# One pool of eight PSUM banks in a fused attention and feed-forward kernel, with the scores in two visits per half batch

## The chip, the cores and the metric

The kernel runs on one core of a Trainium2 chip. The metric is the device time of one launch in microseconds, as the median of several runs. A profile shows one execution; its span runs from the first to the last instruction, some 1.8 us less than the device time.

## The reference, cut to what matters

Attention with a few global and 96 local positions and a linear distance bias, then a feed-forward layer with a squared ReLU:

```python
scores = (q @ k.T) / sqrt(D) + bias          # B, H, S, D = 4, 8, 768, 64
scores = where(is_global | is_local, scores, -1e9)
a = softmax(scores)                          # n_global = 8, n_local = 96
x = (a @ v).transpose(0, 2, 1, 3).reshape(B * S, H * D)      # 3072 x 512
out = square(maximum(x @ w_in, 0)) @ w_out   # 512 -> 2048 -> 512
```

## The kernel before

The kernel works in eight half batches of 384 rows. While TensorE (PE in the profile) does the two feed-forward layers of one half batch, it does the attention of the next between them. Its results go to the banks of PSUM, eight in all in this program: `sp` are scores, `av` is attention times v, `hps` and `yps` are the sums of layer 1 and layer 2, `trp` and `trx` are transposes. ACT takes the exp of scores (`ex`), DVE multiplies by a mask (`phat`), both empty the layers' sums. An attend job is the attention times v of one pair of heads, a load is a DMA transfer into the core, and a filler is a matmul on zeros that the planner puts into gaps of the opening. The first 45 us, until the first layer-2 matmul, are called the opening here: loads arrive, and the first batch is done tile by tile.

The program's order is made ahead of time by a small planner. It is given each job with a cost and what it needs, and emits instructions in the order in which they could start. PSUM stood in two pools, which the planner took each in rotation:

```python
ps_big = ctx.enter_context(tc.tile_pool(name="ps_big", bufs=6, space=bass.MemoryType.PSUM))
ps_att = ctx.enter_context(tc.tile_pool(name="ps_att", bufs=2, space=bass.MemoryType.PSUM))
plan = Plan(1.0, 24.0)
big, att = Ring(6), Ring(2)      # av, trp, trx take att; scores and both layers take big
```

A unit of scores is 8 matmuls of 64 rows into two banks, one for each head of a pair. A half batch has 5 or 6 units. A job of two units took four banks of the ring of six:

```python
TOGETHER = [[[0, NPAIR], [1, 2], [3]], [[0, 1], [2, 3], [4, 5]]]

def score(x, k):
    ...
    units = [UNITS[x.half][u] for u in TOGETHER[x.half][k]]
    ...
    job = plan.pe(0.182 + 0.062 * 4 * len(units), emit,
                  [o for a in pairs for o in x.qk_ops[a]], [big] * 2 * len(units))
    for u, unit in enumerate(units):
        weigh_unit(x, unit, job, u, sp)
```

`PLACES` says after how many layer jobs each score job and each attend job stands, so score jobs in different places are visits with other matmuls between them.

The softmax here doesn't subtract the row's maximum and nothing guards it: scores larger than these inputs give would overflow.

Of the kernel before, what the change touches and what calls it, by code (L numbers as in the profile page):

```python
# [13 lines left out]
P = 128  # L14
# [16 lines left out]
PLACES = {2: (3, 7, 7, 7, 10, 11, 12, 1, 0, 1, 0),  # L31
          0: (0, 4, 9, 6, 11, 16, 18), 1: (0, 6, 11, 9, 11, 17, 19)}
# [9 lines left out]


class Ring:


    def __init__(self, n):
        self.users = [[] for _ in range(n)]
        self.at = 0

    def take(self):
        users = self.users[self.at % len(self.users)]
        before = list(users)
        users.clear()
        self.at += 1
        return before, users


class Plan:
# [10 lines left out]
    def __init__(self, warm_from, warm_until):  # L70
        self.warm_from, self.warm_until = warm_from, warm_until
        self.queues = {"PE": [], "LOAD": []}
        self.rest = []
        self.free = {e: 0.75 for e in ("ACT", "DVE", "POOL", "SP")}
        self.landed = 4.2
        self.rank = 0

    def pe(self, cost, emit, needs=(), takes=(), lag=0.24):
        frees, users = [], []
        for ring in takes:  # L80
            before, now = ring.take()
            frees += before
            users.append(now)
        self.rank += 1
        op = Op({"PE": cost}, emit, [*needs, *frees], self.rank, lag)
        op.frees, op.users = frees, users
        for u in users:
            u.append(op)
        self.queues["PE"].append(op)
        return op  # L90
# [20 lines left out]
    def ready(self, op):  # L111
        t = 0.0
        for n in op.needs:
            if n.done is None:
                return None
            t = max(t, n.done + self.HOP)
        return t + op.wait

    def run(self):
        order = []  # L120
        while self.rest or any(self.queues.values()):
# [11 lines left out]
            idle = self.free.get(e, self.warm_from)  # L133
            self.free[e] = end
# [11 lines left out]
            if e == "PE" and start < self.warm_until and op.users:  # L146
                self.spare = start - 0.1 - max([idle] + [n.done for n in op.frees])
                self.spare *= 0.5 if start < self.warm_from + 5.0 else 1.0
# [6 lines left out]
def kernel(  # L155
# [37 lines left out]
    ps_big = ctx.enter_context(tc.tile_pool(name="ps_big", bufs=6, space=bass.MemoryType.PSUM))  # L193
    ps_att = ctx.enter_context(tc.tile_pool(name="ps_att", bufs=2, space=bass.MemoryType.PSUM))

    plan = Plan(1.0, 24.0)
    big, att = Ring(6), Ring(2)
# [209 lines left out]
    def turn(x, a):  # L407
        state = {}

        def emit(e):  # L410
            state["ps"] = trp = ps_att.tile([P, 2, HT, P], FP16, name="trp", tag="att")
            warm(trp.rearrange("p i t c -> p (i t c)"))
            for i, st in enumerate((x.sq, x.sk)):
                for t in range(HT):
                    nc.tensor.transpose(out=trp[:, i, t, :], in_=st[:, t, 2 * a:2 * a + 2, :],  # L415
                                        identity=ident)
        job = plan.pe(6 * 0.056, emit, x.q_in + x.k_in + [ident_op], [att])
# [33 lines left out]
    TOGETHER = [[[0, NPAIR], [1, 2], [3]], [[0, 1], [2, 3], [4, 5]]]  # L451

    def score(x, k):
        bt = x.bt
        units = [UNITS[x.half][u] for u in TOGETHER[x.half][k]]
        sp = {}

        def emit(e):
            for u, unit in enumerate(units):
                sp[u] = [ps_big.tile([P, 4, P], FP32, name="sp", tag="big") for _ in range(2)]  # L460
                if u == 0:
                    warm(sp[u][0].rearrange("p i c -> p (i c)"))
                for i, (a, r, before) in enumerate(unit):
                    for h in range(2):
                        rows = slice(h * D, (h + 1) * D)
                        lhsT = (bt.kb[rows, a, r - 2, :] if before and r > 1
                                else bt.qk[rows, 1, r - before, a, :])
                        nc.tensor.matmul(sp[u][h][:, i, :], lhsT=lhsT,  # L468
                                         rhs=bt.qk[rows, 0, r, a, :], start=True, stop=True)
        pairs = sorted({a for unit in units for a, _, _ in unit})  # L470
        job = plan.pe(0.182 + 0.062 * 4 * len(units), emit,
                      [o for a in pairs for o in x.qk_ops[a]], [big] * 2 * len(units))
        for u, unit in enumerate(units):
            weigh_unit(x, unit, job, u, sp)

    def weigh_unit(x, unit, job, u, sp):
        st = {}
        exps = []
        for h in range(2):
            def exp(e, h=h):  # L480
                if h == 0:
                    st["ex"] = phat_p.tile([P, 2, 4, P], FP16, name="ex", tag="ex", bufs=6)
                nc.scalar.activation(out=st["ex"][:, h], in_=sp[u][h], func=AF.Exp, scale=scale)  # L483
            exps.append(plan.add({"ACT": 0.505}, exp, [job] + exps))
            job.users[2 * u + h].append(exps[-1])
# [24 lines left out]
    def attend(x, a):  # L510
# [4 lines left out]
        def emit(e):  # L515
            st["av"] = av = ps_att.tile([P, 2, HT, D + 1], FP32, name="av", tag="att")
            warm(av.rearrange("p e t d -> p (e t d)"))
            for h in range(2):
                for j, before in blocks:
# [8 lines left out]
                      + [bt.vb_ops[t] for t in range(*tiles_before(x))], [att])  # L528
# [25 lines left out]
    def layer1(x, ms, c0=0, c1=HALF, k0=0, k1=NCT):  # L554
# [3 lines left out]
        def emit(e):  # L558
            if x.h2 is None:
                x.h2 = h_p.tile([P, NFT, HALF], FP16, name="h2", tag="h2")  # L560
            if k0 == 0:
                st["ps"] = ps_big.tile([P, 512], FP32, name="hps", tag="big")
                warm(st["ps"])
            for i, m in enumerate(ms):
                for kk in range(k0, k1):
# [7 lines left out]
                      [big] if k0 == 0 else [])  # L573
# [34 lines left out]
    def layer2(x, j, m0):  # L608
        st = x.l2.setdefault(j, {})

        def emit(e):
            if m0 == 0:
                st["ps"] = ps_big.tile([P, 512], FP32, name="yps", tag="big")
            for m in range(m0, m0 + 4):
# [3 lines left out]
                      + [w_out_op[m0 // 4]], [big] if m0 == 0 else [])  # L618
# [15 lines left out]
    def last_layer2(x, j):  # L634
        n = d_model // 2
        r0 = x.hb * HALF + j * P
        for c in range(0, d_model, n):
            st = {}

            def emit(e, c=c, st=st):  # L640
                st["ps"] = ps_big.tile([P, 512], FP32, name="yps", tag="big")
# [7 lines left out]
            job = plan.pe(NFT * (n / 2400 + 0.003), emit, [x.h2_ops[m, j] for m in range(NFT)], [big])  # L649
# [12 lines left out]
    def turn_tile(r, n=1):  # L662
# [4 lines left out]
        def emit(e, pairs, fresh):  # L667
            for i, src in enumerate((x.sq, x.sk)):
                if fresh and i < n:
                    st[i] = ps_big.tile([P, 2, NPAIR, P], FP16, name="trp0", tag="big")  # L670
# [6 lines left out]
        if n == 1:  # L677
            job = plan.pe(0.56, lambda e: emit(e, range(NPAIR), True),
                          [x.q_in[t], x.k_in[t], ident_op], [big])
        else:  # L680
            half = plan.pe(0.56, lambda e: emit(e, (0, 1), True), [*first[::2], ident_op],
                           [big] * 2)
# [25 lines left out]
    def score_tile(r, before):  # L708
# [5 lines left out]
        def emit(e):  # L714
            st["sp", before] = pair = [ps_big.tile([P, NPAIR, P], FP32, name="sp", tag="big")
                                       for _ in range(2)]
# [16 lines left out]
        job = plan.pe(0.182 + NPAIR * 0.07 + added * H * 0.056, emit, needs, [big] * 2)  # L733
# [21 lines left out]
    def attend_tile(r, a0):  # L755
# [3 lines left out]
        def emit(e):  # L759
            st["av", a0] = av = ps_att.tile([P, 2, 2, D + 1], FP32, name="av", tag="att")  # L760
# [11 lines left out]
        job = plan.pe(4 * len(kinds) * 0.035, emit, needs, [att])  # L772
# [12 lines left out]
    def tile_to_x(r, a0):  # L785
        x, t, st = halves[r // HT], r % HT, tiles[r]

        def emit(e):
            if x.xt is None:
                x.xt = h_p.tile([P, NCT, HALF], FP16, name="xt", tag="xt")  # L790
            st["trx", a0] = trx = ps_att.tile([P, 2, P], FP16, name="trx", tag="att")
# [4 lines left out]
        job = plan.pe(2 * 0.07, emit, [st["norm", a0]], [att])  # L796
# [6 lines left out]
    def attention(x):  # L803
# [4 lines left out]
        for a in range(NPAIR):  # L808
            if x.hb == 2:
                jobs.append((places[7 + a], lambda a=a: turn(x, a)))  # L810
            jobs.append((places[3 + a], lambda a=a: attend(x, a)))
            jobs.append((places[3 + a], lambda a=a: to_x_by_dma(x, a)))
# [114 lines left out]
```

## Time and profile before

| | before |
|---|---|
| time | 216.48 us (216.27 to 216.57) |
| span of the profile | 214.7 us |
| PE, DVE, ACT busy | 207.1, 122.0, 119.5 us |
| PE's share of the chain that ended last | 89% |
| PE's matmuls | 1908 |

PE is the bound, so the views to read are those of PE: its waits, the chain of work that ended last, and the starts of its matmuls in the timeline. PE's matmuls overlap, so a matmul's duration says little (a score matmul takes 0.22 us in the trace, and the next one starts 0.028 us later on average); the distance from one start to the next says what it costs. The prediction shows the lines.

### The profile page before, as it was taken

The numbers are of one execution on the slowest core, as the hardware profiler recorded it, in microseconds if no ns is written. First come the engines' busy times: TensorE is split into PE (matmuls) and PEld (weight loads), VectorE is DVE, ScalarE is ACT, GpSimd is POOL, SyncE is SP. The second block draws the span as 40 slices with busy tenths as digits, with TensorE's granted clock in tenths as the row PEclk, the third lists the DMA queues.
The fourth block names the chain that finished last, engine by engine and source line by source line (L and its number), as shares of the span: only waits on it lengthen the run. The fifth ranks groups of instructions, "written<-read, shape, count | busy, mean of one in ns | idle before, by whom it ended". The sixth has DMA issues, their size and how long they took to land.

```text
span 214.7 us, 4782 instructions
## 1 busy us (share of the span) xinstructions
PE 207.1 (96%) x1908; PEld 127.1 (59%) x1908; DVE 122.0 (57%) x343; ACT 119.5 (56%) x241; POOL 66.6 (31%) x82
## 2 busy tenths in 40 slices
PE   6798999999999999999999999999999999999994
PEld 7676989755454565446554565455644665456553
DVE  8498887444473589409870689319870697114300
ACT  6879975645661786148721785148721884137421
POOL 8994633693000950086006800094000000000000
PEclk9999999999999999999999999999999999999999
DMA  6999999999944999499967996299952101320012
GB/s 183 162 175 185 196 206 209 157 154 141 196 130 134 133 152 158 118 110 165 141 110 137 178 112 146 60 148 178 132 114 98 52 0 37 89 98 0 0 53 98
DMA packets 106343, 27.06 MB, mean 126 GB/s; under 512 B 96976, under 2 KB 103376, under 8 KB 106320
## 3 DMA queue, kind: packets, MB, share of 16 engines
q0 software_dynamic: 74944, 13.11, 80.5%
q1 hardware_dynamic: 30320, 13.11, 27.1%
q10 hardware_dynamic: 1056, 0.52, 0.8%
q8 instruction: 15, 0.25, 0.5%
q14 instruction: 8, 0.07, 0.1%
HBM read 27.26 MB, written 6.29 MB: 156 GB/s over the span
## 4 chain that ended last, share of the span: by engine, by line
PE 89%; DVE 3%; DMA 3%; ACT 2%; POOL 2%; issue 0%; POOLq 0%
PE hps L566 39%; PE yps L615 37%; PE sp L468 4%; PE av L525 4%; DMA v<-in_v_dram 3%; PE yps L643 2%; DVE vb L206 1%; POOL sk L316 1%; PE av L767 1%; ACT ph L741 1%; PE trp L415 1%; DVE tm L779 1%; PE trx L794 1%; ACT qk L204 1%; POOL v L316 0%
## 5 line engine op out<-in xcount | busy, mean ns | idle before, releaser
L566 PE MATMUL hps<-xt,w_in_sb 128*128 128x384 f16 (+2 forms) x608 | 89.2, 301 | 0.0
L615 PE MATMUL yps<-w_out_sb,h 128*128 128x512 f16 x368 | 83.0, 379 | 0.0
L566 PEld LDWEIGHTS <-w_in_sb 128*128 128x128 f16 x608 | 53.4, 98 | 26.3
L590 ACT ACTIVATE hr<-hps 128x384 f16<-128x384 f32 (+1 forms) x96 | 49.1, 512 | 18.4 <-PE hps L566 16.6
L615 PEld LDWEIGHTS <-h 128*128 128x128 f16 x368 | 34.9, 98 | 39.0
L204 ACT COPY y<-yps 128x512 f32<-128x512 f32 (+1 forms) x25 | 14.2, 569 | 66.7 <-PE yps L615 60.6
L601 DVE TENSOR_TENSOR h<-hr 128x768 f16<-128x768 f16 (+1 forms) x70 | 35.5, 519 | 22.9 <-ACT hr L590 22.9
L316 POOL DMA_DIRECT2D sq<-in_q_dram x22 | 19.5, 894 | 67.6 <-DMA xt<-tm 65.6
L592 DVE TENSOR_SCALAR hr<-hps 128x384 f16<-128x384 f32 (+1 forms) x26 | 14.6, 562 | 37.4 <-PE hps L566 36.5
L483 ACT ACTIVATE ex<-sp 128x512 f16<-128x512 f32 x66 | 34.1, 610 | 1.2 <-PE sp L468 1.2
L316 POOL DMA_DIRECT2D v<-in_v_dram x24 | 21.8, 934 | 4.4 <-DMA w_out_sb<-in_moe_w_out_dram 3.7
L316 POOL DMA_DIRECT2D sk<-in_k_dram x22 | 19.6, 909 | 5.0 <-DMA w_out_sb<-in_moe_w_out_dram 3.1
L503 DVE TENSOR_TENSOR phat<-ex,mask 128x1024 f16<-128x1024 f16 (+1 forms) x36 | 19.9, 595 | 1.5 <-ACT ex L483 1.5
L535 DVE TENSOR_TENSOR tm<-av,rec 128x384 f16<-128x384 f32 x24 | 13.4, 558 | 0.8
L206 DVE COPY vb<-v 128x520 f16<-128x520 f16 (+1 forms) x32 | 10.6, 331 | 2.7 <-DMA v<-in_v_dram 2.0
L525 PEld LDWEIGHTS <-phat 128*128 128x128 f16 x240 | 9.8, 98 | 3.1
L525 PE MATMUL av<-v,phat 128*128 128x65 f16 x144 | 10.9, 194 | 0.0
L206 DVE COPY kb<-qk 128x96 f16<-128x96 f16 (+4 forms) x56 | 8.3, 205 | 3.8 <-DMA qk<-sk 1.8
L468 PEld LDWEIGHTS <-qk 64*128 64x128 f16 x168 | 6.3, 94 | 6.7 <-issue 5.9
L525 PE MATMUL av<-vb,phat 128*128 128x65 f16 x96 | 10.1, 193 | 0.0
L468 PE MATMUL sp<-qk 64*128 64x128 f16 x168 | 9.8, 218 | 0.4 <-ACT ex L483 0.4
L204 ACT COPY qk<-trp 128x512 f16<-128x512 f16 (+1 forms) x12 | 6.2, 549 | 3.8 <-DVE qk L206 1.6
(66 smaller groups left out, 135.6 us busy)
## 6 DMA issues: line engine op xcount, KB each, us to landing
out_dram<-y SPq DMA_DIRECT2D x23, 256.0 KB, 2.2
v<-in_v_dram POOLq DMA_DIRECT2D x24, 128.0 KB, 6.6
sk<-in_k_dram POOLq DMA_DIRECT2D x22, 128.0 KB, 5.9
sq<-in_q_dram POOLq DMA_DIRECT2D x22, 128.0 KB, 5.3
w_in_sb<-in_moe_w_in_dram POOLq DMA_DIRECT2D x4, 512.0 KB, 10.1
w_out_sb<-in_moe_w_out_dram POOLq DMA_DIRECT2D x4, 512.0 KB, 14.1
y<-in_k_dram ACTq DMA_DIRECT2D x2, 256.0 KB, 4.3
y<-in_q_dram SPq DMA_DIRECT2D x2, 256.0 KB, 3.8
```

Source lines behind the costliest of these rows:

```text
L204: nc.scalar.copy(out=out, in_=in_)
L206: eng(e).tensor_copy(out=out, in_=in_)
L316: dma = nc.gpsimd.dma_start(out=dst, in_=src[x.b, :, r0 + t * P:r0 + (t + 1) * P, :] .rearrange("h p d -> p h d"))
L468: nc.tensor.matmul(sp[u][h][:, i, :], lhsT=lhsT, rhs=bt.qk[rows, 0, r, a, :], start=True, stop=True)
L483: nc.scalar.activation(out=st["ex"][:, h], in_=sp[u][h], func=AF.Exp, scale=scale)
L503: eng(e).tensor_tensor(out=x.phat[a][:, :, t0:t0 + n], op=ALU.mult, in0=st["ex"][:, :, i0:i0 + 2 * n].rearrange("p e (t b) c -> p e t (b c ...
L525: nc.tensor.matmul(av[:, h, j, :], lhsT=lhsT, rhs=rhs, start=not before, stop=before or r == 0)
L566: nc.tensor.matmul(st["ps"][:, i * n:(i + 1) * n], lhsT=w_in_sb[:, kk, m * P:(m + 1) * P], rhs=x.xt[:, kk, c0:c1], start=kk == 0, stop=kk ...
L590: nc.scalar.activation(out=o, in_=i, func=AF.Relu)
L592: eng(e).tensor_scalar(out=o, in0=i, scalar1=0.0, scalar2=None, op0=ALU.max)
L601: eng(e).tensor_tensor(out=x.h2[:, m0:m0 + width, c0:c1], in0=hr, in1=hr, op=ALU.mult)
L615: nc.tensor.matmul(st["ps"], lhsT=x.h2[:, m, j * P:(j + 1) * P], rhs=w_out_sb[:, m, :], start=m == 0, stop=m == NFT - 1)
```

## The change

The intent: let the scores of a half batch be visited twice in place of three times, three units and six banks at a time, which needs more banks than the ring of six could spare. (The third half batch has two visits already; the five after it come down from three.) All eight banks become one pool; the planner gives each job the banks that by its own estimate have been idle longest; and each unit becomes a job of its own in the plan, so that its exps no longer wait there for the whole visit.

```diff
-PLACES = {2: (3, 7, 7, 7, 10, 11, 12, 1, 0, 1, 0),
-          0: (0, 4, 9, 6, 11, 16, 18), 1: (0, 6, 11, 9, 11, 17, 19)}
+PLACES = {2: (3, 7, 7, 9, 10, 11, 1, 0, 1, 0),
+          0: (0, 9, 7, 11, 16, 18), 1: (0, 9, 9, 11, 17, 19)}
...
+    def idle_banks(self, n):
+        idle = [(max([u.done for u in users], default=0.0), i) for i, users in
+                enumerate(self.banks) if all(u.done is not None for u in users)]
+        return sorted(idle)[:n] if len(idle) >= n else None
...
-    ps_big = ctx.enter_context(tc.tile_pool(name="ps_big", bufs=6, space=bass.MemoryType.PSUM))
-    ps_att = ctx.enter_context(tc.tile_pool(name="ps_att", bufs=2, space=bass.MemoryType.PSUM))
+    ps_p = ctx.enter_context(tc.tile_pool(name="ps", bufs=1, space=bass.MemoryType.PSUM))
...
+    def bank(shape, dtype, name, i=0):
+        return ps_p.tile(shape, dtype, name=name, tag=f"ps{plan.now[i]}")
...
-    TOGETHER = [[[0, NPAIR], [1, 2], [3]], [[0, 1], [2, 3], [4, 5]]]
+    TOGETHER = [[[0, NPAIR, 1], [2, 3]], [[0, 1, 2], [3, 4, 5]]]
...
-        job = plan.pe(0.182 + 0.062 * 4 * len(units), emit,
-                      [o for a in pairs for o in x.qk_ops[a]], [big] * 2 * len(units))
+        job = plan.pe(0.182 * fresh + 0.057 * 4, emit,
+                      [o for a in {a for a, _, _ in unit} for o in x.qk_ops[a]], 2)
```

(Every other `ps_big.tile` and `ps_att.tile` becomes `bank(...)`, and the jobs' lists of rings become numbers of banks.)

More of the change, by code (lines that the diff above doesn't have):

```diff
@@ L41, in __init__ @@
         self.wait = 0.0
-class Ring:
-    def __init__(self, n):
-        self.users = [[] for _ in range(n)]
-        self.at = 0
-    def take(self):
-        users = self.users[self.at % len(self.users)]
-        before = list(users)
-        users.clear()
-        self.at += 1
-        return before, users
 class Plan:
@@ L76, in __init__, with pe @@
         self.rank = 0
-    def pe(self, cost, emit, needs=(), takes=(), lag=0.24):
-        frees, users = [], []
-        for ring in takes:
-            before, now = ring.take()
-            frees += before
-            users.append(now)
+        self.banks = [[] for _ in range(8)]
+    def pe(self, cost, emit, needs=(), takes=0, lag=0.24):
         self.rank += 1
-        op = Op({"PE": cost}, emit, [*needs, *frees], self.rank, lag)
-        op.frees, op.users = frees, users
-        for u in users:
-            u.append(op)
+        op = Op({"PE": cost}, emit, needs, self.rank, lag)
+        op.takes, op.users = takes, [[op] for _ in range(takes)]
         self.queues["PE"].append(op)
@@ L116, in ready @@
             t = max(t, n.done + self.HOP)
+        if getattr(op, "takes", 0):
+            banks = self.idle_banks(op.takes)
+            if banks is None:
+                return None
+            t = max(t, banks[-1][0] + self.HOP)
         return t + op.wait
+    def idle_banks(self, n):
+        idle = [(max([u.done for u in users], default=0.0), i) for i, users in
+                enumerate(self.banks) if all(u.done is not None for u in users)]
+        return sorted(idle)[:n] if len(idle) >= n else None
     def run(self):
@@ L133, in run @@
             idle = self.free.get(e, self.warm_from)
+            taken = self.idle_banks(op.takes) if getattr(op, "takes", 0) else []
             self.free[e] = end
@@ L145, in run @@
             self.spare = 0.0
-            if e == "PE" and start < self.warm_until and op.users:
-                self.spare = start - 0.1 - max([idle] + [n.done for n in op.frees])
+            for (_, i), users in zip(taken, op.users if taken else ()):
+                self.banks[i] = users
+            self.now = [i for _, i in taken]
+            if taken and start < self.warm_until:
+                self.spare = start - 0.1 - max(idle, taken[-1][0])
                 self.spare *= 0.5 if start < self.warm_from + 5.0 else 1.0
@@ L192 @@
     y_p = ctx.enter_context(tc.tile_pool(name="yp", bufs=6))
-    ps_big = ctx.enter_context(tc.tile_pool(name="ps_big", bufs=6, space=bass.MemoryType.PSUM))
-    ps_att = ctx.enter_context(tc.tile_pool(name="ps_att", bufs=2, space=bass.MemoryType.PSUM))
+    ps_p = ctx.enter_context(tc.tile_pool(name="ps", bufs=1, space=bass.MemoryType.PSUM))
     plan = Plan(1.0, 24.0)
-    big, att = Ring(6), Ring(2)
+    def bank(shape, dtype, name, i=0):
+        return ps_p.tile(shape, dtype, name=name, tag=f"ps{plan.now[i]}")
     def eng(e):
@@ L410, in emit @@
         def emit(e):
-            state["ps"] = trp = ps_att.tile([P, 2, HT, P], FP16, name="trp", tag="att")
+            state["ps"] = trp = bank([P, 2, HT, P], FP16, "trp")
             warm(trp.rearrange("p i t c -> p (i t c)"))
@@ L416, in emit @@
                                         identity=ident)
-        job = plan.pe(6 * 0.056, emit, x.q_in + x.k_in + [ident_op], [att])
+        job = plan.pe(6 * 0.056, emit, x.q_in + x.k_in + [ident_op], 1)
         def evac(i):
@@ L450, with score_unit @@
     UNITS.append([seq[i:i + 4] for i in range(0, len(seq), 4)])
-    TOGETHER = [[[0, NPAIR], [1, 2], [3]], [[0, 1], [2, 3], [4, 5]]]
+    TOGETHER = [[[0, NPAIR, 1], [2, 3]], [[0, 1, 2], [3, 4, 5]]]
     def score(x, k):
-        bt = x.bt
-        units = [UNITS[x.half][u] for u in TOGETHER[x.half][k]]
-        sp = {}
+        for unit in [UNITS[x.half][u] for u in TOGETHER[x.half][k]]:
+            score_unit(x, unit, unit[0] == UNITS[x.half][TOGETHER[x.half][k][0]][0])
+    def score_unit(x, unit, fresh):
+        bt, sp = x.bt, []
@@ L458, in emit @@
         def emit(e):
-            for u, unit in enumerate(units):
-                sp[u] = [ps_big.tile([P, 4, P], FP32, name="sp", tag="big") for _ in range(2)]
-                if u == 0:
-                    warm(sp[u][0].rearrange("p i c -> p (i c)"))
-                for i, (a, r, before) in enumerate(unit):
-                    for h in range(2):
-                        rows = slice(h * D, (h + 1) * D)
-                        lhsT = (bt.kb[rows, a, r - 2, :] if before and r > 1
-                                else bt.qk[rows, 1, r - before, a, :])
-                        nc.tensor.matmul(sp[u][h][:, i, :], lhsT=lhsT,
-                                         rhs=bt.qk[rows, 0, r, a, :], start=True, stop=True)
@@ L470, in score @@
-        pairs = sorted({a for unit in units for a, _, _ in unit})
-        job = plan.pe(0.182 + 0.062 * 4 * len(units), emit,
-                      [o for a in pairs for o in x.qk_ops[a]], [big] * 2 * len(units))
-        for u, unit in enumerate(units):
-            weigh_unit(x, unit, job, u, sp)
-    def weigh_unit(x, unit, job, u, sp):
+            sp.extend(bank([P, 4, P], FP32, "sp", h) for h in range(2))
+            warm(sp[0].rearrange("p i c -> p (i c)"))
+            for i, (a, r, before) in enumerate(unit):
+                for h in range(2):
+                    rows = slice(h * D, (h + 1) * D)
+                    lhsT = (bt.kb[rows, a, r - 2, :] if before and r > 1
+                            else bt.qk[rows, 1, r - before, a, :])
+                    nc.tensor.matmul(sp[h][:, i, :], lhsT=lhsT, rhs=bt.qk[rows, 0, r, a, :],
+                                     start=True, stop=True)
@@ L477, in weigh_unit @@
+        job = plan.pe(0.182 * fresh + 0.057 * 4, emit,
+                      [o for a in {a for a, _, _ in unit} for o in x.qk_ops[a]], 2)
+        weigh_unit(x, unit, job, sp)
+    def weigh_unit(x, unit, job, sp):
         st = {}
@@ L482, in exp @@
                     st["ex"] = phat_p.tile([P, 2, 4, P], FP16, name="ex", tag="ex", bufs=6)
-                nc.scalar.activation(out=st["ex"][:, h], in_=sp[u][h], func=AF.Exp, scale=scale)
+                nc.scalar.activation(out=st["ex"][:, h], in_=sp[h], func=AF.Exp, scale=scale)
             exps.append(plan.add({"ACT": 0.505}, exp, [job] + exps))
-            job.users[2 * u + h].append(exps[-1])
+            job.users[h].append(exps[-1])
         if unit[0][1] == 0:
@@ L515, in emit @@
         def emit(e):
-            st["av"] = av = ps_att.tile([P, 2, HT, D + 1], FP32, name="av", tag="att")
+            st["av"] = av = bank([P, 2, HT, D + 1], FP32, "av")
             warm(av.rearrange("p e t d -> p (e t d)"))
@@ L527, in attend @@
         job = plan.pe(0.0305 * 2 * len(blocks), emit, x.weighs[a] + x.v_in
-                      + [bt.vb_ops[t] for t in range(*tiles_before(x))], [att])
+                      + [bt.vb_ops[t] for t in range(*tiles_before(x))], 1)
         def norm(e):
@@ L561, in emit @@
             if k0 == 0:
-                st["ps"] = ps_big.tile([P, 512], FP32, name="hps", tag="big")
+                st["ps"] = bank([P, 512], FP32, "hps")
                 warm(st["ps"])
@@ L572, in layer1 @@
                        for o in [x.x_ops.get((a, t), x.x_ops.get(a))]] + [w_in_op[ms[0] // 4]],
-                      [big] if k0 == 0 else [])
+                      int(k0 == 0))
         if k0 == 0:
@@ L612, in emit @@
             if m0 == 0:
-                st["ps"] = ps_big.tile([P, 512], FP32, name="yps", tag="big")
+                st["ps"] = bank([P, 512], FP32, "yps")
             for m in range(m0, m0 + 4):
@@ L617, in layer2 @@
         job = plan.pe(4 * 0.216, emit, [x.h2_ops[m, j] for m in range(m0, m0 + 4)]
-                      + [w_out_op[m0 // 4]], [big] if m0 == 0 else [])
+                      + [w_out_op[m0 // 4]], int(m0 == 0))
         if m0 == 0:
@@ L640, in emit @@
             def emit(e, c=c, st=st):
-                st["ps"] = ps_big.tile([P, 512], FP32, name="yps", tag="big")
+                st["ps"] = bank([P, 512], FP32, "yps")
                 for m in range(NFT):
@@ L648, in evac @@
                 copy(e, st["y"][:, 0:n], st["ps"][:, 0:n])
-            job = plan.pe(NFT * (n / 2400 + 0.003), emit, [x.h2_ops[m, j] for m in range(NFT)], [big])
+            job = plan.pe(NFT * (n / 2400 + 0.003), emit, [x.h2_ops[m, j] for m in range(NFT)], 1)
             y_op = plan.after(job, {"ACT": 0.3, "DVE": 0.35}, evac)
@@ L669, in emit @@
                 if fresh and i < n:
-                    st[i] = ps_big.tile([P, 2, NPAIR, P], FP16, name="trp0", tag="big")
+                    st[i] = bank([P, 2, NPAIR, P], FP16, "trp0", i)
                     if i == 0:
@@ L678, in turn_tile @@
             job = plan.pe(0.56, lambda e: emit(e, range(NPAIR), True),
-                          [x.q_in[t], x.k_in[t], ident_op], [big])
+                          [x.q_in[t], x.k_in[t], ident_op], 1)
         else:
-            half = plan.pe(0.56, lambda e: emit(e, (0, 1), True), [*first[::2], ident_op],
-                           [big] * 2)
+            half = plan.pe(0.56, lambda e: emit(e, (0, 1), True), [*first[::2], ident_op], 2)
             job = plan.pe(0.56, lambda e: emit(e, (2, 3), False), first[1::2])
@@ L714, in emit @@
         def emit(e):
-            st["sp", before] = pair = [ps_big.tile([P, NPAIR, P], FP32, name="sp", tag="big")
-                                       for _ in range(2)]
+            st["sp", before] = pair = [bank([P, NPAIR, P], FP32, "sp", i)
+                                       for i in range(2)]
             warm(pair[0].rearrange("p a c -> p (a c)"))
@@ L732, in score_tile @@
             needs += [kb_ops[r - 1]] if r > 1 else tile_ops[r - 1]
-        job = plan.pe(0.182 + NPAIR * 0.07 + added * H * 0.056, emit, needs, [big] * 2)
+        job = plan.pe(0.182 + NPAIR * 0.07 + added * H * 0.056, emit, needs, 2)
         exps = []
@@ L759, in emit @@
         def emit(e):
-            st["av", a0] = av = ps_att.tile([P, 2, 2, D + 1], FP32, name="av", tag="att")
+            st["av", a0] = av = bank([P, 2, 2, D + 1], FP32, "av")
             warm(av.rearrange("p a e d -> p (a e d)"))
@@ L771, in attend_tile @@
             needs.append(bt.vb_ops[r - 1] if r > 1 else bt.v_in[0])
-        job = plan.pe(4 * len(kinds) * 0.035, emit, needs, [att])
+        job = plan.pe(4 * len(kinds) * 0.035, emit, needs, 1)
         def norm(e):
@@ L790, in emit @@
                 x.xt = h_p.tile([P, NCT, HALF], FP16, name="xt", tag="xt")
-            st["trx", a0] = trx = ps_att.tile([P, 2, P], FP16, name="trx", tag="att")
+            st["trx", a0] = trx = bank([P, 2, P], FP16, "trx")
             warm(trx.rearrange("p i c -> p (i c)"))
@@ L795, in emit @@
                                     identity=ident)
-        job = plan.pe(2 * 0.07, emit, [st["norm", a0]], [att])
+        job = plan.pe(2 * 0.07, emit, [st["norm", a0]], 1)
         op = plan.after(job, {"ACT": 0.29, "DVE": 0.25}, lambda e: copy(
@@ L809, in attention @@
             if x.hb == 2:
-                jobs.append((places[7 + a], lambda a=a: turn(x, a)))
-            jobs.append((places[3 + a], lambda a=a: attend(x, a)))
-            jobs.append((places[3 + a], lambda a=a: to_x_by_dma(x, a)))
+                jobs.append((places[6 + a], lambda a=a: turn(x, a)))
+            jobs.append((places[2 + a], lambda a=a: attend(x, a)))
+            jobs.append((places[2 + a], lambda a=a: to_x_by_dma(x, a)))
         return sorted(jobs, key=lambda j: j[0])
```

## The prediction

> **What bounds the kernel now.** I read first the page's busy shares and its chain that ended last, then TensorE's waits over the whole run, then the chain and the timeline of single stretches.
>
> ```profile
> PE 207.1 (96%) x1908; PEld 127.1 (59%) x1908; DVE 122.0 (57%) x343; ACT 119.5 (56%) x241; POOL 66.6 (31%) x82
> PE 89%; DVE 3%; DMA 3%; ACT 2%; POOL 2%; issue 0%; POOLq 0%
> ```
>
> TensorE (PE) is busy for 96% and carries 89% of the chain; DVE and ACT have more than 40% to spare. What PE still loses shows in its waits (total, times, longest, in us):
>
> ```profile
> PE av L767 <- ACT xt L204: 0.9, 2, 0.5
> PE sp L468 <- ACT ex L483: 0.4, 1, 0.4
> PE av L767 <- DVE xt L206: 0.3, 1, 0.3
> ```
>
> The L767 waits lie in the opening, between 15 and 19 us. After 21.5 us the only wait listed is the 0.4 us at L468. So a gain after the opening must come from that one wait or from how PE's own instructions stand. The chain in one half batch of the steady part (start, us, what):
>
> ```profile
> 118.65 0.55 PE sp L468 x16
> 119.20 4.01 PE hps L566 x24
> 123.21 0.55 PE sp L468 x16
> ...
> 127.48 0.55 PE sp L468 x16
> 128.04 0.47 PE av L525 x12
> 128.51 3.25 PE hps L566 x20
> ```
>
> Three score jobs (sp) of 16 matmuls stand between layer-1 matmuls (hps). The 20 hps not followed by scores take 3.25 us, 0.1625 each; 24 at that pace would be 3.90, but the 24 that end at a score job take 4.01. And at the other edge, PE's timeline:
>
> ```profile
> 118.92 0.22 PE L468 MATMUL sp<-qk 64*128 64x128 f16 x2
> 118.98 0.22 PE L468 MATMUL sp<-qk,kb 64*128 64x128 f16 x2
> 119.13 4.07 PE L566 MATMUL hps<-xt,w_in_sb 128*128 128x384 f16 x24
> ```
>
> Score matmuls start in pairs 0.057 us apart (0.028 each), but the first full-height matmul starts 0.15 after the last pair, 0.095 more. Together a visit to the scores costs 0.11 + 0.095 = 0.20 us beyond its matmuls, whatever their number: 16 x 0.028 + 0.095 = 0.55, as the chain has it.
>
> The one wait after the opening, in the chain:
>
> ```profile
> 58.51 0.34 PE sp L468 x7
> 58.85 0.02 issue
> 58.87 0.61 ACT ex L483
> 59.48 0.04 issue
> 59.52 0.38 PE sp L468 x7
> ```
>
> A job of 24 stops in its middle. The neighbours in the timeline start at 58.90 and 59.52, so 0.62 in place of 0.05: 0.57 us lost. The exp it waits for reads the first of this same job's banks: the job takes six banks of a ring of six, and the layer-2 output just before holds one of them, so its last unit must reuse a bank that it has itself just filled.
>
> **What the Trainium skill says.** "TensorEngine Tiling (Array Packing)", section "Tiling Modes": "Changing tiling mode (not just tile) drains the TensorE". The scores are 64-row matmuls (64*128 in the rows above) between 128-row ones, so this is the fixed cost; the trace agrees and gives its size, 0.20 us for in and out. "Perfetto Trace Analysis", section "Matmul Optimizations": all eight banks should be used for the most parallelism; in its section "Optimization Strategy" (under identifying opportunities), consistent bubbles can mean that PSUM ran out. The trace agrees for four places only: the waits above, each for a bank's reader; the steady part has no such bubble. "PSUM — Partial Sum Buffer", "Specifications (TRN2)": eight banks of 2 KiB. So three units of two banks leave two for everything else; no run yet shows whether that is enough.
>
> **The change part by part.**
>
> 1. Fewer visits to the scores. By the order of the built programs, matmul counts and the opening's PE sequence are the same. From the third half batch on, before has 2, 3, 3, 3, 3, 3 score visits (16+24; then 16+16+16 or 16+16+8), after 2, 2, 2, 2, 2, 2 (24+16 or 24+24). That is 5 visits fewer, 5 x 0.20 = 1.0 us. All of it is on PE, where the steady part has no idle time, so it comes off the end whole.
>
> 2. The stop in the third half batch. After, the 24 come first and the 16 after the layer-2 matmuls. The 24 need six of eight banks; the order shows the waits of its last unit on transposes' banks emptied before. The 16 start some 0.75 + 3.5 us later and wait for banks of the first three exps or so. Six exps at 0.49 us (six took 3.04 with the last one's tail) are done 3.0 us after the first starts. So this stop goes: 0.57 us. No new one by this count.
>
> 3. The opening. The second attend job waits for a bank of the ring of two (0.52 idle in the timeline at 16.16), another at 17.94 (0.27), another at 19.01 (0.34): 1.13 us. In the new program these three wait for data or for long emptied banks. But the gain is not theirs to keep. ACT is busy without a break from 14.76 to 25.9, in an order that is unchanged up to about 23:
>
> ```profile
> 17.61 0.59 ACT L204 COPY qk<-trp 128x512 f16<-128x512 f16 x1
> 18.28 0.40 PE L728 MATMUL sp<-qk 64*128 64x128 f16 x8
> 19.01 0.19 PE L767 MATMUL av<-v,ph 128*128 128x65 f16 x1 [0.34 <-ACT xt L204]
> ```
>
> The scores at 18.28 need that ACT copy, which does not come sooner, so the first two waits (0.79) are given back there. The third (0.34) can be kept. Next the load of the fourth quarter of w_in (it lands at 25.98) gates the hps at 26.40, so no more than some 0.4 can pass. I take 0.35 us.
>
> 4. ACT and DVE. The new plan puts nine instructions more on ACT and nine fewer on DVE. At 0.5 us each, ACT goes from 119.5 to some 124, still under 60%. Exps freed by unit are a matter of the plan's bookkeeping: on the chip ACT waited for the tiles that it reads already. No cost, no gain.
>
> Sum: 1.0 + 0.57 + 0.35 = 1.9 us; 216.48 - 1.9 = 214.6.
>
> **The rivals.**
>
> A: banks run short behind the 24. Behind them ACT has one y copy and six exps, 7 x 0.49 = 3.4 us, and only two banks are outside the scores. Against it: layer 1 takes a bank every 4 x 0.1625 = 0.65 us, the exps give one back every 0.49, DVE can empty an hps in 0.56, and the order shows the third hps waiting for the first exp and the fourth for the third: due 1.3 and 1.95 us after the first hps starts. In the stretch above the exps started at 119.17; with 0.23 us more of scores the hps would start at 119.36, the first exp end at 119.77 (0.4 in), the third at 119.17 + 0.98 + 0.6 = 120.75 (1.4 in). Behind the second visit it is tighter: there ACT first has the relu of the last hps (0.49), and the attend job after two hps (due 0.37 + 1.30 = 1.7 us after the scores end) waits for the third exp, by the same count about 1.45 in. That margin of some 0.25 is thin. If it fell short at each of the ten score visits by 0.2 to 0.3, part 1 would be eaten: 216.6 to 217.6.
>
> B: the whole 1.13 us of the opening is kept, if the copy on ACT can move forward after all: 213.8. Against it stands ACT's unbroken row.
>
> C: the opening gives nothing, because its next wait (weights, transposes of the last tile, ACT) takes it all: 214.9. And if the stop of part 2 turns up elsewhere too: 215.5.
>
> D: attention becomes late. The attend jobs of pair 0 and 1 come later in odd half batches (9 for 6), and their transposed output must land before the next layer 1. Against it: the last attend keeps its place (19), and in the third half batch the last output landed at 69.35, with its first reader at 71.2.
>
> **Range and chances.** The first part is sure by count (within 0.1), the second nearly; the third is 0 to 0.6; rival A costs at most what is gained, at 1 in 10. That gives 213.9 to 215.5. 2% would be 212.15, 2.4 us below my estimate, more than every lost time on PE that I found put together; so faster has 1 in 100. Slower by 2% would need 4 us of new waits: 2 in 100.
>
> **What would show each step right or wrong.** In the profile after: two score pieces per half batch in the chain, 24 of them taking 24 x 0.028 + 0.095 = 0.78 us, with 0.1 us lost in the hps ahead of each; no wait L468 on ACT ex; the three L767 waits gone, yet the scores of about 18.28 at the same time within 0.1; the hps of 26.40 at about 26.05. A stretch of 24 us from 118 on should hold some 0.2 us more work of the same list. I am wrong if PE's waits list hps or sp behind ACT ex with tenths of a microsecond at each score visit (rival A), if the opening gives over 0.7 us (B), or if hps wait for the transposed xt (D).

## The result, and the profile after

| | before | after |
|---|---|---|
| time, 5 runs each | 216.57 us (216.27 to 216.61) | 214.38 us (214.35 to 214.51) |
| ratio of fast runs | | 0.9904, 95% interval 0.9889 to 0.9918 |
| span | 214.7 us | 212.7 us |
| opening: start of the first layer-2 matmul | 45.12 us | 44.88 us |
| steady part: from there to the last half batch's first layer-1 matmul | 145.49 us | 143.80 us |

A ratio is the mean time of one kernel's fast runs over that of the other's of the same rounds, so it is not quite the ratio of the medians. The change gains 1%. That is under the 2% at which the record speaks of "faster", but the interval leaves no doubt of the sign. The time lies inside the range of 213.9 to 215.5.

The page after, busy shares and the chain's shares by engine:

```profile
PE 206.0 (97%) x1908; PEld 127.3 (60%) x1908; DVE 116.7 (55%) x334; ACT 122.0 (57%) x250; POOL 66.6 (31%) x82
PE 93%; DMA 3%; POOL 1%; DVE 1%; ACT 0%; issue 0%; POOLq 0%
```

The number of matmuls is the same. PE carries more of the chain; but the part outside PE fell by some 9 us (11% of 214.7 to 7% of 212.7), far more than the 2 us gained, so this share does not measure the gain. PE's waits after, the whole run (total, times, longest, in us):

```profile
PE trp L216 <- DVE ident L239: 1.7, 1, 1.7
PE trp L669 <- DMA sq<-in_q_dram: 1.0, 1, 1.0
PE sp L721 <- ACT qk L200: 0.4, 1, 0.4
PE trp L669 <- DVE sq L202: 0.3, 1, 0.3
PE trp L669 <- ACT sk L200: 0.2, 1, 0.2
```

The bank waits on `av`, and the wait of `sp` on ACT's exp, are gone. All that is left lies in the opening and waits for data. The chain after, in the stretch that the prediction showed of before (start, us, what):

```profile
117.36 0.78 PE sp L464 x24
118.13 5.96 PE hps L560 x36
124.09 0.78 PE sp L464 x24
124.87 0.47 PE av L519 x12
125.34 1.30 PE hps L560 x8
```

Two visits of 24, each 0.78 us as estimated, and 36 layer-1 matmuls in 5.96 us: 36 x 0.1625 + 0.11. And in the third half batch, where before stopped inside a job, the second visit now runs through:

```profile
58.49 0.55 PE sp L464 x16
59.04 0.41 PE av L519 x10
```

### The profile page after: what moved, and what is told of

Same layout as the page of the kernel before. It is cut to its first block, busy times and chain, and to the rows that moved or that the text cites. A ratio compares the mean times of both kernels' runs of the same rounds, so it can differ in the third digit from the quotient of the medians.

```text
span 212.7 us, 4804 instructions
## 1 busy us (share of the span) xinstructions
PE 206.0 (97%) x1908; PEld 127.3 (60%) x1908; DVE 116.7 (55%) x334; ACT 122.0 (57%) x250; POOL 66.6 (31%) x82
## 4 chain that ended last, share of the span: by engine, by line
PE 93%; DMA 3%; POOL 1%; DVE 1%; ACT 0%; issue 0%; POOLq 0%
PE hps L560 40%; PE yps L609 37%; PE sp L464 4%; PE av L519 4%; DMA sq<-in_q_dram 3%; PE yps L637 2%; PE sp L721 2%; PE av L760 1%; PE sp L714 1%; PE trp L669 1%; PE trx L787 1%; PE trp L411 1%; POOL v L312 0%; POOL sk L312 0%; DVE tm L772 0%; ACT qk L200 0%
## 5 line engine op out<-in xcount | busy, mean ns | idle before, releaser
L584 ACT ACTIVATE hr<-hps 128x384 f16<-128x384 f32 (+1 forms) x106 | 54.9, 526 | 14.4 <-PE hps L560 13.3
L477 ACT ACTIVATE ex<-sp 128x512 f16<-128x512 f32 x66 | 35.0, 621 | 1.2 <-PE sp L464 1.2
L586 DVE TENSOR_SCALAR hr<-hps 128x384 f16<-128x384 f32 (+1 forms) x16 | 9.0, 562 | 39.4 <-PE hps L560 39.4
L202 DVE COPY vb<-v 128x520 f16<-128x520 f16 (+1 forms) x32 | 9.9, 309 | 1.6 <-DMA v<-in_v_dram 0.9
L464 PE MATMUL sp<-qk 64*128 64x128 f16 x168 | 8.8, 218 | 0.0
L527 DVE RECIPROCAL rec<-av 128x6 f32<-128x6 f32 x24 | 4.7, 194 | 7.0 <-PE av L519 6.6
```

What stands on the lines that cost most here:

```text
L202: eng(e).tensor_copy(out=out, in_=in_)
L464: nc.tensor.matmul(sp[h][:, i, :], lhsT=lhsT, rhs=bt.qk[rows, 0, r, a, :], start=True, stop=True)
L477: nc.scalar.activation(out=st["ex"][:, h], in_=sp[h], func=AF.Exp, scale=scale)
L584: nc.scalar.activation(out=o, in_=i, func=AF.Relu)
```

## The experiments

xt_on_dve_look is the kernel of xt_on_dve_w once more. "Opening" and "steady" are as above, read from the starts of PE's matmuls in each run's trace. The kernel before had medians of 216.45 to 216.59 us.

| run | us | ratio to before | opening | steady |
|---|---|---|---|---|
| after_again | 214.36 | 0.9904 | 44.74 | 143.80 |
| regroup_old_pools | 218.26 | 1.0082 | 45.17 | 147.22 |
| pool_only | 215.48 | 0.9955 | 44.80 | 144.87 |
| ring_of_8 | 214.51 | 0.9910 | 45.00 | 143.80 |
| visits_by_unit | 218.25 | 1.0076 | 44.72 | 147.64 |
| banks_7 | 214.47 | 0.9905 | 44.84 | 143.80 |
| banks_6 | 219.37 | 1.0127 | 45.29 | 148.07 |
| xt_on_dve | 215.66 | 0.9953 | 46.05 | 143.80 |
| xt_on_dve_w | 215.48 | 0.9945 | slow profile | slow profile |
| xt_on_dve_look | 215.50 | 0.9942 | 45.85 | 143.80 |
| g01_first | 214.36 | 0.9894 | 44.73 | 143.80 |
| pools_7_1 | 225.04 | 1.0390 | 52.07 | 146.85 |

The steady part repeats to 0.01 us wherever PE does not wait in it, so differences of 0.1 us there are real. The opening is another matter: the two profiles of the changed kernel differ by 0.14 us there (44.88 and 44.74).

### after_again: the changed kernel beside the others

No edit.

> The changed kernel once more, so that the others of this call stand beside it on one chip. Expected 214.4 us, 2.1 us under the kernel before. The profile is to tell whether the loads of the first tiles, which landed some 0.55 us later in the profile of after than in that of before, differ from run to run (then here either value) or by the change (then again the later one).

Measured: 214.36 us. The first load of k, for which the others stand, landed at 4.51 us in the profile of before, 5.07 in that of after, and 4.65 here (4.53 to 4.82 in the eleven others). So it differs from run to run and is not the change's doing.

### regroup_old_pools: the grouping without the pool

```diff
 (kernel before, with the new PLACES and TOGETHER, and the two new offsets into PLACES)
-    TOGETHER = [[[0, NPAIR], [1, 2], [3]], [[0, 1], [2, 3], [4, 5]]]
+    TOGETHER = [[[0, NPAIR, 1], [2, 3]], [[0, 1, 2], [3, 4, 5]]]
```

> The new grouping and places alone, on the old pools of six and two banks; the order of PE's matmuls is exactly that of the changed kernel. Theory (the pool makes the three-unit visit possible): a visit takes all six banks of its pool, so its last unit waits for the copy of the bank just filled and the layer after it for the first exp, about 0.5 us at each of ten visits; 1.0 us is saved by the visits: about 216.5 - 1.0 + 5 = 220, certainly over 217.5, with waits of PE sp and hps on ACT. Rival (only the number of visits counts, the pool is decoration): 215.5, no such waits.

Measured: 218.26 us, slower than the kernel before. PE's matmuls stand in exactly the order of the changed kernel, so only the banks differ. The chain around one visit of 24 behind layer 2, and the next behind layer 1:

```profile
119.39 0.58 ACT y L204
119.97 0.51 ACT ex L483
120.48 0.04 issue
120.53 6.01 PE hps L566 x36
126.54 0.96 PE sp L468 x24
```

The visit, which takes 0.78 us in the changed kernel, has vanished from the chain behind ACT: its last unit waits for ACT to copy out the last layer-2 sum, and the layer-1 matmuls behind it wait for the first exp. The second visit takes 0.96: its last unit starts when ACT has emptied the last layer-1 sum ahead of it (126.57 to 127.06). In the starts of the matmuls the stops inside visits sum to 2.35 us at nine places (0.59 of it in the third half batch, as before), and five waits behind visits add 0.93. The direction is the theory's. The sum is not: 0.26 and 0.19 us at the five visits behind layer 2 (inside and behind, together near the 0.5 expected), but only 0.16 at the three behind layer 1, and none where a visit has 16 matmuls, in place of 0.5 at ten visits. The rival, that only the number of visits counts, is out.

### pool_only: the pool without the grouping

```diff
 (changed kernel, with the old PLACES, TOGETHER and offsets)
-    TOGETHER = [[[0, NPAIR, 1], [2, 3]], [[0, 1, 2], [3, 4, 5]]]
+    TOGETHER = [[[0, NPAIR], [1, 2], [3]], [[0, 1], [2, 3], [4, 5]]]
```

> The shared pool of eight alone, with the old grouping and places (two-unit jobs, exps by unit). Theory: it keeps what the opening gave (0.25) and the stop in the third half batch (0.57), and lacks the 5 visits saved (1.0): 216.5 - 0.8 = 215.7, 1.0 to 1.3 over the changed kernel. Rival (the pool is the main part of the gain): 214.6 or less.

Measured: 215.48 us, 1.12 over after_again. The steady part is 144.87: 0.62 less than before, which is the stop in the third half batch, and 1.07 more than after, which is five visits. The opening has its gain already. This one run splits the change into its three parts, and each agrees with the prediction.

### ring_of_8: one pool, but in rotation

```diff
 (regroup_old_pools, with one pool)
-    ps_big = ctx.enter_context(tc.tile_pool(name="ps_big", bufs=6, ...
-    ps_att = ctx.enter_context(tc.tile_pool(name="ps_att", bufs=2, ...
+    ps_big = ctx.enter_context(tc.tile_pool(name="ps_big", bufs=8, ...
+    ps_att = ps_big
-    big, att = Ring(6), Ring(2)
+    big = att = Ring(8)
```

> One pool of eight banks, but taken in strict rotation, with the new grouping; PE's order of matmuls is that of the changed kernel. Theory A (eight shared banks are what counts, the choice by idle time little): within 0.6 us of the changed kernel, 214.4 to 215.0. Theory B (the choice of the banks idle longest counts): the rotation meets banks still held by a layer-2 sum or by exps, tenths of a us at each visit: 216 or more.

Measured: 214.51 us, 0.15 over after_again, with overlapping intervals; the steady part is the same to 0.01 us. Since it is built on the kernel before, it also keeps the old bookkeeping of exps by whole visits; so this one run covers that part of the change too. In its profile the opening ends 0.26 us later than that of after_again, but the load of w_in that gates it landed 0.25 us later too (26.23 against 25.98), so that is no sign of the rotation. Theory A holds: choosing the banks idle longest gains nothing that these runs can show, nor do exps by unit. The opposite choice (the banks idle for the shortest time) was not run.

### visits_by_unit: the price of a visit

```diff
-          0: (0, 9, 7, 11, 16, 18), 1: (0, 9, 9, 11, 17, 19)}
+          0: (0, 3, 6, 9, 11, 7, 11, 16, 18), 1: (0, 3, 6, 9, 11, 13, 9, 11, 17, 19)}
...
-    TOGETHER = [[[0, NPAIR, 1], [2, 3]], [[0, 1, 2], [3, 4, 5]]]
+    TOGETHER = [[[0], [NPAIR], [1], [2], [3]], [[0], [1], [2], [3], [4], [5]]]
```

> The changed kernel with each unit of scores of the last five half batches visited by itself: 6 and 5 visits in place of 2, 18 visits more in all, same matmuls, same pool. Theory (a visit costs 0.20 us whatever it holds): 214.4 + 18 x 0.20 = 218.0, and PE still has no waits in the steady part. Rival (the visits are free, the gain was from waits): 214.4 to 214.8.

Measured: 218.25 us. The chain in the steady part:

```profile
118.70 0.33 PE sp L464 x8
119.03 2.06 PE hps L560 x12
121.08 0.33 PE sp L464 x8
121.41 2.06 PE hps L560 x12
123.47 0.33 PE sp L464 x8
```

A visit of 8 takes 0.33 us, one of 24 0.78: 0.028 a matmul and 0.105 fixed; and 12 layer-1 matmuls ahead of a visit take 2.06, 0.11 over 12 x 0.1625. The steady part grew by 147.64 - 143.80 = 3.84 us, over 18 visits 0.213 each. PE waits for nothing in it. So the price of a visit is a fixed 0.21 us, and the rival (visits are free) is out. It is not the price of every change of work: in the steady part of the profile of after, attend and layer-2 matmuls (128 rows, like layer 1) start 0.162 us behind the last layer-1 matmul, the usual distance, while the first score matmul (64 rows) starts 0.259 behind it.

### banks_7 and banks_6: how many banks it takes

```diff
-        self.banks = [[] for _ in range(8)]
+        self.banks = [[] for _ in range(7)]      # 6 in banks_6
```

> The changed kernel with seven banks in the pool. It asks how near the eight are to too few. Theory: a visit of six leaves one bank, and the layer behind it gets its second from the copy of the sum before the visit, in time or late by 0.1 to 0.2 us: 214.4 to 216, my middle 215.0. If rival A of the prediction (eight are barely enough) is nearly true, 216 or more.

> The changed kernel with six banks in the pool: a visit of three units takes all. Theory: PE stops at each of the ten three-unit or so visits for 0.5 to 1 us, and at attends: 219 to 224. If banks hardly matter: under 216.

Measured: with seven banks 214.47 us, and a steady part equal to that with eight. With six 219.37: the same stops as in regroup_old_pools inside and behind visits (2.35 and 0.93 us), and more at the attend jobs. So the step lies between six and seven: the largest job's six and one. Eight are not barely enough, as rival A had it; one bank is spare.

### pools_7_1: seven banks, but not shared

```diff
 (regroup_old_pools; the lines of the pools shortened)
-    ps_big bufs=6, ps_att bufs=2;  big, att = Ring(6), Ring(2)
+    ps_big bufs=7, ps_att bufs=1;  big, att = Ring(7), Ring(1)
-            x.qk_ops[a] = x.turned + [plan.add(*fix_k(x, a), x.turned[:1], wait=4.0)]
+            x.qk_ops[a] = x.turned + [plan.add(*fix_k(x, a), x.turned[:1], wait=7.0)]
```

> The new grouping on two separate pools again, of seven banks and one in place of six and two (one DVE copy is planned 3 us later, else the build reads it before it is written; three fillers fewer). Theory (in the steady part only the size of the pool of the scores and layers counts, not that it is shared; sharing matters in the opening): from the first layer-2 matmul to the last layer 1 PE takes 143.8 us as in the changed kernel, within 0.1, while the opening, with one bank for attends and their transposes, loses 0.5 to 2 us: 215 to 216.5. Rival (sharing counts everywhere): stops at the attends of the steady part too, over 217.

Measured: 225.04 us. The steady part as defined is 146.85, so the expectation as written fell. But the loss lies in one place: from the first score visit of the fourth half batch to the last half batch's first layer-1 matmul it takes 118.92 us (80.00 to 198.92), and the changed kernel 118.89 (69.79 to 188.68). The other 3.0 us are lost in the third half batch, whose transposes on PE I had forgotten: they and the attends queue for the one bank. The opening loses 7.3 us in the same way, well over the 2 expected. Of PE's waits, the first line here lies in the third half batch and the other two in the opening:

```profile
PE trp L415 <- ACT qk L204: 1.9, 2, 1.0
PE trx L794 <- ACT xt L204: 1.8, 2, 1.4
PE av L767 <- DVE tm L779: 1.6, 3, 0.7
```

Part of the opening's loss is a second effect. After PE had been busy for only 1.39 of the 3.00 us from 18 on, its clock was halved for 3.4 us, from 21.08 to 24.49. PE was busy for 3.1 us of that, so at the full clock some 1.6 us would have been saved at most (an estimate, from these two figures). The windows view (stretch, its length, then busy time of PE, PEld, DVE, ACT and POOL, each with its count, PE's clock, DMA share, GB/s):

```profile
18.00:21.00 3.00, 1.39 (x23) 0.91 (x20) 1.46 (x6) 1.85 (x4) 0.74 (x1) 1.00 1.88 175
21.00:24.50 3.50, 3.12 (x39) 2.75 (x39) 2.69 (x9) 1.08 (x2) 2.51 (x4) 0.51 1.60 195
```

The Trainium skill, "TensorE: Matmul & The Clock Gate", section "What's actually happening", gives such a half-rate state after an idle window of some 3.4 us. The trace agrees on the half rate. Here PE was not idle all that time: it was busy for half of the 3.41 us before the clock fell (1.71 us), and its longest wait in that time was 1.4 us. That this stretch brought the clock down is inferred from the order of events in one profile.

So in the last five half batches only the size of the pool of scores and layers counts. Sharing counts where attends and transposes come close together.

### xt_on_dve, xt_on_dve_w, xt_on_dve_look: what holds the opening back

```diff
-        op = plan.after(job, {"ACT": 0.29, "DVE": 0.25}, lambda e: copy(
+        op = plan.after(job, {"DVE": 0.25}, lambda e: copy(
 (and, in the last two)
-    plan = Plan(1.0, 24.0)
+    plan = Plan(1.0, 14.0)
```

> The changed kernel with the opening's copies of xt on DVE alone, so that ACT has up to six copies of 0.25 us less between 15 and 32 us. Theory (ACT's row gates the scores near 18.4 us, and the load of the fourth quarter of w_in that lands near 25.9 us gates the rest): those scores some 0.2 us earlier, but the end at most 0.25 us earlier: 214.2 to 214.4. Rival B of the prediction (only ACT held the opening back): 213.7.

> The opening's xt copies on DVE alone again, but with the plan's filler matmuls on zeros limited to the first 14 us, so that their number is the 60 of the changed kernel. In xt_on_dve the plan had put 15 more of them between 19.9 and 23.4 us (0.67 + 0.67 us of PE's time), which hid what was asked. Theory (the load of the last but one quarter of w_in gates the end of the opening): 214.2 to 214.5. Rival B of the prediction (only ACT held the opening back): 213.7.

> The same kernel as xt_on_dve_w, whose profiled execution fell in a slow one (clock 0.66), while its other runs agreed at 215.48, 1.1 us over the changed kernel, against both theories. Wanted: where in the opening that 1.1 us goes. If DVE has become the bound there, PE waits for DVE (trx, av or hps after a DVE row) before 30 us and the start of layer 2 comes at about 45.9 in place of 44.8; the stretch from there to the last layer 1 stays 143.8. If the steady part has changed, that stretch is longer.

Measured: 215.66, 215.48 and 215.50 us. All are 1.1 to 1.3 us slower than the changed kernel, where both theories had expected a small gain. The first also had 15 filler matmuls more (1923 matmuls in place of 1908). The second had its profile taken in an execution of 307.47 us at a clock of 0.66; its other five agree at 215.45 to 215.50. The third shows the cause; its PE has the same matmuls in the same order as the changed kernel. PE's waits in its opening:

```profile
PE sp L721 <- ACT ex L734: 0.6, 1, 0.6
PE hps L560 <- DVE xt L202: 0.4, 1, 0.4
PE trx L787 <- DVE tm L772: 0.2, 1, 0.2
```

Its chain from 17.96 to 23.10 us consists of DVE's rows and 0.04 us of issue, and the layer-1 job that needs the last xt copy starts at 23.15. From 18 to 23 us DVE was busy for 4.93 us, where after_again had 4.32 (and ACT 5.00): DVE has become the bound. The scores meant to start earlier started at 18.44. So the copies' division between ACT and DVE in the changed kernel is not slack to be taken, and this experiment does not answer what it was made for.

### g01_first: the landing of w_in

```diff
-X10 S4b X20 ... S5o G30 G31 S5b A41 G01 F3 X30 G21 ...
+X10 S4b X20 ... S5o G01 G30 G31 S5b A41 F3 X30 G21 ...
```

> The changed kernel with one layer-1 job of the opening that needs weights long landed (G01) put ahead of those that wait for the fourth landing of w_in. In three profiles PE stood 0.1 to 0.3 us there. If that landing is what caps the opening, the start of layer 2 (44.74 to 44.88) comes 0.1 to 0.3 us earlier: 214.1 to 214.3. If the next stage (exps of the last tile, then its attends) is as tight, no change: 214.4.

Measured: 214.36 us, and the opening ends at 44.73 where after_again had 44.74. The ratio, 0.9894, is 0.001 under that of after_again, within both intervals. No gain shows. In its profile PE came to this place 0.2 us later than in after_again, for reasons earlier in the opening, and had no wait there to lose; so whether the new order helps stays open.

What gates the opening is seen best in after_again's chain:

```profile
13.94 0.83 POOL v L312
14.77 11.21 DMA w_in_sb<-in_moe_w_in_dram
25.98 0.05 issue
26.02 1.92 PE hps L560 x16
```

The job of 16 starts 0.04 us after the load of w_in lands. In pool_only (26.03 and 26.08) and ring_of_8 (26.23 and 26.27) it is the same. In the profile of after it landed at 25.91 and the job started at 26.16, because PE came late itself; in visits_by_unit, banks_7 and g01_first, too, PE reached this job (26.00 to 26.12) without a wait for the load.

No version beat the changed kernel.

## Why the prediction was right

The predicted 214.6 us was measured as 214.38. By its own steps, which sum to 2.04 us as measured (the ratio gives 2.1):

1. **Fewer visits, 1.0 us: right.** pool_only against the changed kernel gives 1.07 us in the steady part for the five visits, and visits_by_unit gives 0.213 us a visit, in place of 0.20. The missing 0.01 is in the first pairs of a visit, which stand slightly wider apart than later ones. Nothing else in the steady part moved.

2. **The stop in the third half batch, 0.57 us: right.** Before against pool_only is 0.62 us. The stop returns as soon as a visit of six has only six banks (0.59 us in regroup_old_pools and in banks_6).

3. **The opening, 0.35 us: right in sum, with noise of the same order.** Two profiles with the old pools' opening end it at 45.12 and 45.17 us; five with the new pool's (after, after_again, pool_only, visits_by_unit, banks_7) at 44.72 to 44.88, mean 44.80. That the first two bank waits, 0.79 us, would be given back to ACT's copy is borne out: over the same two and five profiles the scores behind them start at 18.30 and 18.22 us on average, and in all five ACT's `qk` copy is what ends PE's idle time there (0.40 and 0.15 us in the two profiles of the changed kernel). The third wait is gone for good: the attend behind these scores starts 0.73 us after them with the old pools, 0.33 with the new. The load of w_in as the next gate is shown in three profiles; in four others PE came just too late to wait for it. What failed is the fine check in single profiles: the scores of 18.28 were to stay within 0.1 us, and stood at 18.42 and 18.02. The first landings differ by up to half a microsecond between runs, which a comparison of two single profiles cannot see past.

4. **ACT and DVE, no cost: right, and mis-sized.** Nine instructions went to ACT, as counted, but its busy time rose from 119.5 to 122.0, not to 124. It is far from the bound in either case. That freeing exps by unit gains nothing is borne out by ring_of_8, which does not have it and has the same steady part (143.80 us).

**Rival A** (banks run short) did not happen; with seven banks nothing changes, with six it does, by 5 us. **B** (1.13 us from the opening) and **C** (nothing) are out by the mean of 0.35. **D** (attention late) is out, since PE waits for no xt after the opening. My closing check by a stretch of 24 us from 118 on shows little: the half batches stand 1.3 us earlier there (first scores at 117.29 for 118.58), so it does not hold the same list of work.

What the prediction left open was how much of the change's machinery is needed. The grouping needs the pool: on the old pools it loses 0.8%, while the pool alone gains 0.45%, and together they gain 0.96%. And of the pool only its size matters in the last five half batches.

## What to carry to other kernels

When PE is the bound and no wait is left, look at the joints where matmuls of another height begin and end: here each visit to 64-row matmuls costs 0.21 us whatever it holds, so fewer and larger visits pay. To make a visit larger, its pool needed the banks of the largest job and one more (here six and one); sharing all eight paid where short users come close together, and the rule that picks a bank made no difference beside a plain rotation. A job that takes every bank of its pool waits for the reader of the sum ahead of it, and the work behind it waits for its own first reader.

## What the Trainium skill lacked or had wrong

- "TensorEngine Tiling (Array Packing)", "Tiling Modes", says that changing the mode drains TensorE, and gives no time: here 0.11 us going in and 0.105 coming out, 0.213 a visit over 18 added visits. That this time is the drain is not shown; that it is fixed, and that the joints between 128-row matmuls do not have it, is.
- "Perfetto Trace Analysis", "Matmul Optimizations", asks for all eight PSUM banks. Seven and eight gave the same steady part to 0.01 us (143.80), six gave 148.07: what counted was the largest job's banks and one.
- "TensorE: Matmul & The Clock Gate", "What's actually happening", ties the half rate to an idle window of some 3.4 us, and does not say how little work makes a window idle. In pools_7_1 PE was busy for 1.71 of the 3.41 us that came before 3.41 us at half clock.
- No page tells of a program on a single core held at one low clock of about two thirds from start to end: one of the six of xt_on_dve_w took 307.47 us at a mean clock of 0.66, the other five some 215.5.
